# Pooled attention with a feed-forward block: the first batch's steps reordered, its value product turned round

## The chip, the cores and the metric

The kernel runs on one core of one Trainium2 chip. The metric is the device time of one execution in microseconds (us), lower is better; times of several executions are given as their median. TensorE is called PE (its weight loads PEld), VectorE DVE, ScalarE ACT, GpSimd POOL; SP is the engine whose queue issues nearly all DMAs.

## The reference

Four batches of eight heads, 1152 rows of 64 elements. The queries are averaged in pairs, the attention of 576 queries on 1152 keys is formed, and the result goes through a layer norm and a two-layer block with a hidden width of 2048.

```python
q_pool = q.reshape(B, H, S // 2, 2, D).mean(axis=3)
scores = 1.0 / np.sqrt(D) * np.matmul(q_pool, k.transpose(0, 1, 3, 2))
scores = scores - np.max(scores, axis=-1, keepdims=True)
attn = np.exp(scores)
attn = attn / (np.sum(attn, axis=-1, keepdims=True) + 1e-09)
x = np.matmul(attn, v)              # heads side by side: (4, 576, 512)
mu = np.mean(x, axis=-1, keepdims=True)
var = np.mean((x - mu) ** 2, axis=-1, keepdims=True)
xn = (x - mu) / np.sqrt(var + 1e-06) * g_ln
out = x + np.maximum(xn @ w_ch1, 0.0) @ w_ch2
```

## The kernel before

**Steps.** Heads are taken in 16 pairs, each pair in 9 steps of 128 pooled queries, which makes 144 steps. Step i of the main loop (function `step`) issues, in an order written out by hand, a piece of several steps at once: the row maximum of step i (`emit_max`, DVE, line 337), the scores of step i+1 (`emit_s`, PE, line 324: nine matmuls into the three PSUM banks of slot (i+1) mod 2, which are banks 0 to 2 or 3 to 5), the exponential of step i (`emit_exp`, ACT, line 343), the product with V of an earlier step (`emit_pv`, PE) and its evacuation (`evac_pv`: `one` takes the reciprocal of the row sums on DVE, lines 446 to 449, `two` scales the result on ACT, line 453), and one preparation of the next pair's K or Q (`prep_k`, `prep_q`: PE transposes, then a high half by ACT, line 264, and a low half by DVE, line 265). What an engine is given it runs in that order.

**Two ways to turn P.** The product with V needs the exponentials transposed. Steps 36 to 143 do that with a DMA. Steps 0 to 35, the first batch (`on_pe`), do it on PE: `emit_t` (line 376) transposes nine 128x128 float32 blocks back into the banks that held the scores, and `emit_t_copy` (line 382, ACT, in the next step) copies them to SBUF in two parts. `emit_pv` (line 400) then multiplies in float32, with the transposed exponentials as the weight (128x128) and V with a column of ones (65 columns) as what streams through. Each such matmul shows in the trace as two weight loads and two matmuls, so that a step has 18 of each, or 36 in the step that spans two heads. The result goes to columns 128 to 258 of the last bank of slot (i+1) mod 2, the bank into which the scores of step i+1 have just been written.

**Beside it.** The float32 weights of the feed-forward block come in 32 pieces during the first 32 steps: `w_load(m)` (a 512 KB DMA on SP, line 633) in step m, `w_bias` (ACT, line 638) at the end of step m+1, `w_conv` (three DVE operations, queued in `fill` and issued at line 106) from step m+3, `w_sums` (PE, line 665) in even steps, `w_reduce` after every eighth piece. Then `w_splits` has POOL turn them into two float16 parts (lines 238 and 721). `bound` (line 179) and `all_max` (lines 194 to 203) find the scales of a pair's Q, K and V; their PSUM place is the same bank as the result's, in columns 258 to 386. The feed-forward units start some steps after step 36, one to a step (two from step 149 on), and the last 90 us of the span hold little else.

Of the kernel before, what the change touches and what calls it, by code (L numbers as in the profile page):

```python
# [24 lines left out]
def tile_pooled_attention_moe(  # L25
# [93 lines left out]
    def load_q(p, engs, us=(0, 1)):  # L119

        if 0 in us:
            r = raw_p.tile([128, 2, C, 2, D], FP32, tag="qr", name="qr")
        else:
            r = raws[p, "q"]
        for u in us:
            b, hp = divmod(p + u, HP)
            for h in range(2):
                engs[(2 * u + h) % len(engs)].dma_start(  # L128
                    out=r[64 * u:64 * u + 64, h],
                    in_=q[b, 2 * hp + h].rearrange("(p c r) d -> p c r d", c=C, r=2),  # L130
                )
            raws[p + u, "q"] = r
# [51 lines left out]
    def all_max(src, n, then):  # L184

        mx = sm_p.tile([3, 1], FP32, tag="mx3", name="mx3")
        dg = sm_p.tile([3, 3], FP32, tag="dg", name="dg")

        def place():
            return psum[:, 3 * (pv_slot[0] % 2) + 2, 258:386]  # L190

        def one():
            ps = place()
            nc.tensor.transpose(ps[0:n], src, ident)

            def evac():
                nc.vector.tensor_reduce(mx[0:n], ps[0:n], axis=AX.X, op=ALU.max)
                nc.vector.tensor_scalar(dg[0:n, 0:n], ident[0:n, 0:n], mx[0:n], None, op0=ALU.mult)
            return evac

        def two():
            ps = place()
            nc.tensor.matmul(out=ps[:, 0:n], lhsT=ones3[0:n], rhs=dg[0:n, 0:n], start=True, stop=True)
            return lambda: then(ps[:, 0:n])

        return one, two


    reds = deque()

    def scales_reduce(p, a=0, b=3, then=None):
        def end(ps):
# [45 lines left out]
        scaled(vr[:, h], vr[:, h], s)  # L258
        nc.gpsimd.tensor_tensor(vt[:, :, 66:66 + D], vr[:, h], vt[:, :, 0:D], op=ALU.subtract)

    def split_from(ps, s, hi, lo):

        return (
            lambda: nc.scalar.activation(out=hi, in_=ps, func=ACTF.Copy, scale=s),
            lambda: nc.vector.scalar_tensor_tensor(lo, ps, s, hi, op0=ALU.mult, op1=ALU.subtract),  # L265
        )

    def prep_k(p, u):

        kr, kt, s = raws[p, "k"], kt_of(p), pair[p]["s"]  # L270
        ps = bank()
        if u < 2:
            for m in range(4):
                x = kr[:, u, 2 * m:2 * m + 2].rearrange("p c d -> p (c d)")
                nc.tensor.transpose(ps[:, 128 * m:128 * m + 128], x, ident)
            return split_from(ps, s[:, 0:1], kt[:, 0, u, 0:512], kt[:, 1, u, 0:512])
        for h in range(2):
            nc.tensor.transpose(ps[0:64, 128 * h:128 * h + 128], kr[:, h, C - 1], ident)
        x = ps[0:64, 0:256].rearrange("p (h n) -> p h n", h=2)
        return split_from(x, s[0:64, 0:1], kt[0:64, 0, :, 512:640], kt[0:64, 1, :, 512:640])  # L280

    def prep_q(p, u):

        o = 64 * (p % 2)
        qr = raws[p, "q"][o:o + 64].rearrange("p h c r d -> p (h c) (r d)")
        qt, s = qt_of(p), pair[p]["s"]
        ps = bank()
        for m in range(6):
            nc.tensor.transpose(  # L289
                ps[:, 64 * m:64 * m + 64], qr[:, 6 * u + m], ident[o:o + 64, o:o + 64]  # L290
            )
        c = slice(384 * u, 384 * u + 384)
        return split_from(ps[:, 0:384], s[:, 1:2], qt[:, 0, c], qt[:, 1, c])

    PREPS = ((prep_k, 0), (prep_k, 2), (prep_q, 0), (prep_q, 1), (prep_k, 1), (prep_q, 2))

# [14 lines left out]
    def emit_s(i):  # L311
# [3 lines left out]
        if j == 4:  # L315
            parts = [(h, h * C * 64 + 512, 64, 64 * h) for h in range(2)]
        else:
            h = 0 if j < 4 else 1
            parts = [(h, h * C * 64 + 128 * (j if h == 0 else j - 5), 128, 0)]
        for a, (ka, qa) in enumerate(((0, 0), (1, 0), (0, 1))):  # L320

            for r, c0, n, k0 in ((64, 0, 512, 0), (0, 512, 512, 0), (0, 1024, 128, 512)):
# [61 lines left out]
    def emit_pv(i, ps=None):  # L384
# [10 lines left out]
            parts = [(0 if j < 4 else 1, 0, 128, ps[:, 0:65])]  # L395
        if on_pe(i):
            pt = pt.rearrange("p a n -> p (a n)").bitcast(FP32)
            for h, q0, w, dst in parts:
                for u, c in enumerate(ORDER):
                    nc.tensor.matmul(  # L400
                        out=dst, lhsT=pt[:, 128 * u + q0:128 * u + q0 + w], rhs=vt[:, h, c],
                        start=(u == 0), stop=(u == C - 1),
                    )
            return ps
        for h, q0, w, dst in parts:
            for u, c in enumerate(ORDER):
                x = vt[:, h, c]
                hi, lo = pt[:, u, q0:q0 + w], pt[:, C + u, q0:q0 + w]
                for lhsT, rhs in ((hi, x[:, 0:65]), (hi, x[:, 66:130]), (lo, x[:, 0:65])):
# [5 lines left out]
                        skip_group_check=True,  # L415
                    )
        return ps

    pv_slot = [0]
    xb, xh = {}, {}  # L420
# [221 lines left out]
    def w_conv(m):  # L642
# [12 lines left out]
            nc.vector.scalar_tensor_tensor, xi, hi, SIGN, lo,  # L655
            op0=ALU.bitwise_and, op1=ALU.bitwise_or,
        )
        later(lambda: sums.append(lambda: w_sums(part, 2 * c + z, lo)))

    def w_sums(part, u, mag):  # L660

# [8 lines left out]
    def w_reduce(part):  # L670
        while fill:
            drip()
        while sums:
            sums.popleft()()
        m = wmax[:, part:part + 1]
        if part % 2 == 0:

# [54 lines left out]
    def pre(i, fn, *a):  # L732
        early.setdefault(i, []).append((fn, a))

    for p in range(1, NP):
        i0 = (p - 1) * C
        at(max(i0 - 1, 0), load, p, "k", nc.sync)
        at(i0, load, p, "v", nc.sync)
        at(i0 + 1, bound, p, "k")
        if p % 2 == 0:  # L740
            at(i0 - 1, load_q, p, (nc.sync,))
            pre(i0 + 1, pool_q, p, nc.gpsimd)
            at(i0 + 1, dup_q, p, nc.gpsimd)
            at(i0 + 2, bound, p, "q")
        elif p == 1:
            upper = (64, 64)
            pre(0, lambda: nc.gpsimd.memset(state(1)["acc"][0:64, 1:2], 0.0))
            pre(i0 + 1, pool_q, 1, nc.gpsimd, (upper,))
            at(i0 + 1, dup_q, 1, nc.gpsimd, (upper,))
            at(i0 + 2, bound, 1, "q", *upper)  # L750
# [5 lines left out]
        for n in range(2):  # L756
            at(i0 + (5, 7)[n], take_v, p, n)
        for n, (fn, u) in enumerate(PREPS):
            pre(i0 + (4, 5, 6, 6, 7, 8)[n], lambda fn=fn, p=p, u=u: preps.append((fn, p, u)))

    for m in range(32):
        i0 = m
        pre(i0, w_load, m)
        at(i0 + 1, w_bias, m)
        pre(i0 + 3, w_conv, m)
        if m % 8 == 7:
            at(i0 + 3, w_reduce, m // 8)

    this = [0]

# [83 lines left out]
        ready.setdefault(max(n + (2 if on_pe(n) else 4), 3), []).append(n)  # L854
    pieces = deque()

    def some_units(i):
        if preps:
            fn, p, u = preps.popleft()
            evacs.extend(fn(p, u))  # L860
        for _ in range(1 if i < NSTEP + 5 else 2):
            if units and w_done[units[0][0]] >= units[0][1]:
                evacs.extend(units.popleft()[2]())

    def a_piece(i):
        pieces.extend(ready.pop(i, ()))
        for u in range(2 if len(pieces) > 2 else 1):
            if pieces:
                n = pieces.popleft()
                ps = emit_pv(n, bank() if u else None)  # L870
                evacs.extend(evac_pv(n, ps))
                evacs.append(lambda n=n: evacuated(n))

    def step(i):
# [6 lines left out]
        if on_pe(i - 1):  # L881
            emit_t_copy(i - 1)
            steps.pop(i - 1)
        if i + 1 < NSTEP:
            emit_s(i + 1)
            pv_slot[0] = i + 1
        else:
            free_banks[:] = [6, 7, 0, 1, 3, 4]
            pv_slot[0] += 1
        while sums and i % 2 == 0:  # L890
            sums.popleft()()
        flush()
        if live:
            emit_exp(i)
            if not on_pe(i):
                emit_hi(i)
        if 0 <= i - 1 < NSTEP and not on_pe(i - 1):
            emit_lo(i - 1)
# [2 lines left out]
        norm(i)  # L901
        while soon or len(fill) > 3:
            drip()
        if reds:
            evacs.append(reds.popleft()())
        a_piece(i)
        some_units(i)
        if live and on_pe(i):
            emit_t(i)
        for fn, a in todo.pop(i, ()):  # L910
            fn(*a)

    with tc.manual_schedule():
# [14 lines left out]
        make_identity(nc, ident)  # L928
        nc.gpsimd.tensor_copy(ident16, ident)

        for _ in range(70):
            nc.tensor.matmul(out=psum[:, 2, 0:128], lhsT=ident16, rhs=ident16, start=True, stop=True)
        st = state(0)
        nc.vector.memset(st["acc"], 0.0)
# [64 lines left out]
```

## Time and profile before

| | us |
|---|---|
| median of 3 runs | 969.31 (957.99, 969.43, 969.31) |
| span of the profiled execution, first to last instruction | 963.9 |
| PE busy in the span | 880.9 (91%) |
| DVE busy | 627.4 (65%) |
| ACT busy | 549.9 (57%) |
| POOL busy | 346.4 (36%) |
| granted TensorE clock, mean | 0.938 of full speed |

The span is that of one execution under the profiler; the device times of the runs also hold what lies before its first and after its last instruction. No device time is given for the profiled execution itself. Times in the trace count from the span's start. A granted clock of 1.00 is 2.4 GHz and 0.50 is 1.2 GHz.

### The profile page before, as it was taken

What the parts mean: (1) busy time and instruction counts of PE and PEld (TensorE: products, weight loads), DVE (VectorE), ACT (ScalarE), POOL (GpSimd) and SP (SyncE); (2) the same over time, 40 slices, a digit from 0 to 9 for tenths busy, and PEclk for the clock granted to TensorE, in tenths of its full rate; (3) what the DMA queues carried; (4) which work ended last, traced back from release to release, by engine and by line L of the source; (5) the groups of instructions that cost most, each with busy time, mean ns of one, the idle gap of its engine ahead of it and who ended that gap; (6) DMA issues with size and microseconds to landing.
All of it is one profiled execution on the core that took longest, in us unless ns stands there. A gap on an engine that the chain in (4) does not pass through costs nothing.

```text
span 963.9 us, 21832 instructions
## 1 busy us (share of the span) xinstructions
PE 880.9 (91%) x9286; PEld 628.5 (65%) x9286; DVE 627.4 (65%) x1160; ACT 549.9 (57%) x779; POOL 346.4 (36%) x315
## 2 busy tenths in 40 slices
PE   5897988999869899989698999999989999999998
PEld 4676766777747476666474757566765766767665
DVE  4576696767787577757875777678777777542221
ACT  3765465655476677667667677676676766411000
POOL 3002165243579352435543424344534241310000
PEclk7897797968889999999999999999999999999999
DMA  5325152150155988698959596969596886600000
GB/s 156 145 70 183 66 177 69 48 183 1 50 99 106 191 125 171 129 197 133 179 102 209 102 198 129 187 131 174 101 208 118 168 143 116 122 23 12 12 12 22
DMA packets 271665, 114.92 MB, mean 119 GB/s; under 512 B 254928, under 2 KB 254928, under 8 KB 271568
## 3 DMA queue, kind: packets, MB, share of 16 engines
q1 hardware_dynamic: 271216, 112.65, 56.2%
q8 instruction: 72, 1.18, 0.5%
q10 hardware_dynamic: 352, 0.88, 0.3%
q14 instruction: 25, 0.20, 0.1%
HBM read 45.09 MB, written 4.72 MB: 52 GB/s over the span
## 4 chain that ended last, share of the span: by engine, by line
PE 57%; DVE 20%; ACT 9%; DMA 7%; issue 3%; SPq 3%; POOL 0%; ACTq 0%; DVEq 0%; POOLq 0%
PE psum L534 14%; PE psum L565 14%; PE psum L324 8%; PE psum L400 7%; PE psum L411 7%; DVE mx L337 5%; DMA pt<-hl 4%; DVE hl L366 4%; ACT pt L382 3%; PE psum L376 3%; DMA stage<-in_moe_w_ch_dram 2%; DVE ht L548 2%; PE psum L289 2%; SPq L128 2%; DVE kt L265 1%
## 5 line engine op out<-in xcount | busy, mean ns | idle before, releaser
L337 DVE TENSOR_REDUCE mx<-psum 128x1 f32<-128x1152 f32 x144 | 194.4, 1350 | 76.6 <-PE psum L400 39.6
L343 ACT ACTIVATE pe<-psum,nb,sc 128x1152 f32<-128x1152 f32 x144 | 188.9, 1312 | 29.5 <-DVE nb L338 28.2
L565 PE MATMUL psum<-wsl,ht 128*128 128x512 f16 x864 | 199.0, 383 | 0.2 <-DVE ht L548 0.2
L324 PE MATMUL psum<-kt,qt 64*128 64x512 f16 (+3 forms) x1440 | 166.3, 342 | 28.2 <-ACT pt L382 17.0
L534 PEld LDWEIGHTS <-wsl 128*128 128x128 f16 x1920 | 172.8, 99 | 25.1 <-issue 3.0
L534 PE MATMUL psum<-xn,wsl 128*128 128x256 f16 x1536 | 181.2, 277 | 2.1 <-DVE xn L504 1.1
L324 PEld LDWEIGHTS <-qt 64*128 64x128 f16 (+1 forms) x1440 | 70.6, 99 | 114.4 <-issue 76.0
L565 PEld LDWEIGHTS <-ht 128*128 128x128 f16 x864 | 82.5, 99 | 92.2 <-issue 4.3
L357 ACT ACTIVATE hl<-pe 128x1152 f16<-128x1152 f32 x108 | 125.7, 1164 | 19.5 <-DMA pt<-hl 16.2
L453 ACT ACTIVATE xb<-psum,r 128x64 f32<-128x64 f32 x128 | 40.1, 313 | 150.6 <-DVE r L449 142.1
L411 PEld LDWEIGHTS <-pt 128*128 128x128 f16 (+1 forms) x3240 | 108.9, 101 | 22.6 <-issue 22.1
L411 PE MATMUL psum<-vt,pt 128*128 128x65 f16 (+1 forms) x3240 | 120.5, 195 | 0.0
L366 DVE SCALAR_TENSOR_TENSOR hl<-pe,hl 128x1152 f16<-128x1152 f32 x72 | 104.9, 1457 | 0.0
L238 POOL TENSOR_SCALAR pe<-pe 128x1152 f32<-128x1152 f32 x36 | 42.0, 1166 | 153.9 <-ACT hl L357 143.6
L548 DVE SCALAR_TENSOR_TENSOR ht<-psum,ht 128x512 f16<-128x512 f32 x72 | 49.6, 690 | 72.6 <-ACT ht L547 71.8
L547 ACT ACTIVATE ht<-psum 128x512 f16<-128x512 f32 x72 | 42.8, 594 | 93.7 <-PE psum L534 93.3
L400 PE MATMUL psum<-vt,pt 128*128 128x65 f32 (+1 forms) x720 | 96.1, 298 | 0.0
L400 PEld LDWEIGHTS psum<-vt,pt 128*128 128x128 f32 (+1 forms) x720 | 91.9, 213 | 3.6 <-issue 3.4
L364 POOL TENSOR_TENSOR hl<-pe,hl 128x1152 f16<-128x1152 f32 x36 | 85.4, 2373 | 3.0
L382 ACT COPY pt<-psum 128x512 f32<-128x512 f32 x72 | 44.7, 639 | 55.9 <-PE psum L376 55.1
L161 POOL TENSOR_TENSOR qr<-qr 128x1152 f32<-128x1152 f32 (+1 forms) x8 | 22.3, 2786 | 130.2 <-DMA qr<-in_q_dram 94.6
L376 PE MATMUL psum<-ident,pe 128*128 128x128 f32 x324 | 51.7, 315 | 5.1 <-ACT pe L343 4.9
(104 smaller groups left out, 898.6 us busy)
## 6 DMA issues: line engine op xcount, KB each, us to landing
stage<-in_moe_w_ch_dram SPq DMA_DIRECT2D x32, 512.0 KB, 6.7
kr<-in_k_dram SPq DMA_DIRECT2D x16, 576.0 KB, 4.4
qr<-in_q_dram SPq DMA_DIRECT2D x31, 288.0 KB, 5.6
vr<-in_v_dram SPq DMA_DIRECT2D x15, 576.0 KB, 5.0
out_dram<-xb SPq DMA_DIRECT2D x32, 128.0 KB, 2.5
pt<-hl SPq DMA_TRANSPOSE x108, 4.8
vr<-in_v_dram ACTq DMA_DIRECT2D x1, 576.0 KB, 6.1
out_dram<-xh SPq DMA_DIRECT2D x4, 128.0 KB, 3.5
```

Source lines behind the costliest of these rows:

```text
L324: nc.tensor.matmul(out=sp[o:o + w, c0:c0 + n], lhsT=qt[r:r + 64, qa, q0:q0 + w], rhs=kt[r:r + 64, ka, h, k0:k0 + n], start=(a == 0), stop= ...
L337: nc.vector.tensor_reduce(mx, st["s"], axis=AX.X, op=ALU.max)
L343: nc.scalar.activation(out=st["pe"], in_=st["s"], func=ACTF.Exp, scale=pair[i // C]["sc"][:, 0:1], bias=st["nb"],)
L357: nc.scalar.activation(out=hl[:, 0], in_=st["pe"], func=ACTF.Copy, scale=2.0 ** 15)
L364: nc.gpsimd.tensor_tensor(hl[:, 1], st["pe"], hl[:, 0], op=ALU.subtract)
L366: nc.vector.scalar_tensor_tensor(hl[:, 1], st["pe"], 2.0 ** 15, hl[:, 0], op0=ALU.mult, op1=ALU.subtract)
L376: nc.tensor.transpose(st["s"][:, n], st["pe"][:, n], ident)
L382: nc.scalar.copy(st["pt"][:, a:b], st["s"][:, a:b])
L400: nc.tensor.matmul(out=dst, lhsT=pt[:, 128 * u + q0:128 * u + q0 + w], rhs=vt[:, h, c], start=(u == 0), stop=(u == C - 1),)
L411: nc.tensor.matmul(out=dst[:, 0:n], lhsT=lhsT, rhs=rhs, start=(u == 0 and lhsT is hi and n == 65), stop=(u == C - 1 and lhsT is lo), skip_ ...
L534: nc.tensor.matmul(out=ps[:, o:o + n], lhsT=wsl[:, 8 * w + cc, wa, f * 128:f * 128 + 128], rhs=xn[:, xa * KD + cc, 0:n], start=(m == 0), s ...
L565: nc.tensor.matmul(out=ps, lhsT=hv[0][:, ha, f, t * 128:t * 128 + 128], rhs=wsl[:, 8 * w + 4 + f // 2, wa, (f % 2) * DM:(f % 2) * DM + DM] ...
```

## The change

In the first batch's steps the order becomes: product with V of an earlier step, a preparation, the exponential, the scores of step i+1, and then `emit_t`. Columns 0 to 65 of V are now the weight of the product and the transposed exponentials stream through; its result, 65 rows by 128 queries, goes to one of the two spare banks (6 and 7), ACT copies it to SBUF (`nc.scalar.copy(ot, ...)`), and `emit_turn` transposes it on PE into the last bank of slot i mod 2. The reciprocal of that result is taken in the next step behind the maximum (`found`), and the scaling behind the next step's exponential (`scaled_out`). The sums of the weights go to PE in the step in which their bank is that of the scores of step i+1; the bounds go to the bank of slot i. The raw queries get two buffers and are loaded a step earlier; the weights' bias comes two steps later, their conversion one, their reduction one or two. A POOL copy that reads the first pair's scales is put ahead of POOL's first memset in the loop. 110 small matmuls run ahead of the first data, not 70. Assertions and the set `have` add no instruction.

```diff
         if 0 in us:
-            r = raw_p.tile([128, 2, C, 2, D], FP32, tag="qr", name="qr")
+            r = raw_p.tile([128, 2, C, 2, D], FP32, tag="qr", name="qr", bufs=2)
         else:
             r = raws[p, "q"]
...
         def place():
-            return psum[:, 3 * (pv_slot[0] % 2) + 2, 258:386]
+            u = this[0] if on_pe(this[0]) else pv_slot[0]
+            return psum[:, 3 * (u % 2) + 2, 258:386]
 
         def one():
...
-    reds = deque()
+    reds, found = deque(), deque()
 
     def scales_reduce(p, a=0, b=3, then=None):
...
         if on_pe(i):
             pt = pt.rearrange("p a n -> p (a n)").bitcast(FP32)
-            for h, q0, w, dst in parts:
+            for h, q0, w, _ in parts:
                 for u, c in enumerate(ORDER):
                     nc.tensor.matmul(
-                        out=dst, lhsT=pt[:, 128 * u + q0:128 * u + q0 + w], rhs=vt[:, h, c],
+                        out=ps[0:65, q0:q0 + w], lhsT=vt[:, h, c],
+                        rhs=pt[:, 128 * u + q0:128 * u + q0 + w],
                         start=(u == 0), stop=(u == C - 1),
                     )
...
                     )
         return ps
+
+    turned, scaled_out = deque(), deque()
+
+    def emit_turn(n, ot, i):
+
+        j = n % C
+        ps = psum[:, 3 * (i % 2) + 2, 128:258]
+        parts = [(h, 64 * h, 64) for h in range(2)] if j == 4 else [(0, 0, 128)]
+        for h, q0, w in parts:
+            nc.tensor.transpose(ps[0:w, 65 * h:65 * h + 65], ot[:, q0:q0 + w], ident[0:65, 0:65])
+        one, two = evac_pv(n, ps)
+        found.append(one)
+        scaled_out.extend((two, lambda: evacuated(n)))
 
     pv_slot = [0]
...
             op0=ALU.bitwise_and, op1=ALU.bitwise_or,
         )
-        later(lambda: sums.append(lambda: w_sums(part, 2 * c + z, lo)))
+        later(lambda: sums.append((part, lambda: w_sums(part, 2 * c + z, lo))))
 
     def w_sums(part, u, mag):
...
             drip()
         while sums:
-            sums.popleft()()
+            sums.popleft()[1]()
         m = wmax[:, part:part + 1]
         if part % 2 == 0:
...
         early.setdefault(i, []).append((fn, a))
 
+    def behind_scales():
+        nc.gpsimd.tensor_copy(state(1)["acc"][0:64, 1:2], state(0)["sc"][0:64, 0:1])
+        nc.gpsimd.memset(state(1)["acc"][0:64, 1:2], 0.0)
+
     for p in range(1, NP):
         i0 = (p - 1) * C
...
         at(i0 + 1, bound, p, "k")
         if p % 2 == 0:
-            at(i0 - 1, load_q, p, (nc.sync,))
+            at(i0 - 2, load_q, p, (nc.sync,))
             pre(i0 + 1, pool_q, p, nc.gpsimd)
             at(i0 + 1, dup_q, p, nc.gpsimd)
...
         elif p == 1:
             upper = (64, 64)
-            pre(0, lambda: nc.gpsimd.memset(state(1)["acc"][0:64, 1:2], 0.0))
+            pre(0, behind_scales)
             pre(i0 + 1, pool_q, 1, nc.gpsimd, (upper,))
             at(i0 + 1, dup_q, 1, nc.gpsimd, (upper,))
...
             at(i0 + (5, 7)[n], take_v, p, n)
         for n, (fn, u) in enumerate(PREPS):
-            pre(i0 + (4, 5, 6, 6, 7, 8)[n], lambda fn=fn, p=p, u=u: preps.append((fn, p, u)))
+            late = 1 if on_pe(i0) else 0
+            pre(i0 + (4, 5, 6, 6, 7, 8)[n] + late, lambda fn=fn, p=p, u=u: preps.append((fn, p, u)))
 
     for m in range(32):
         i0 = m
         pre(i0, w_load, m)
-        at(i0 + 1, w_bias, m)
-        pre(i0 + 3, w_conv, m)
+        at(i0 + 3, w_bias, m)
+        pre(i0 + 4, w_conv, m)
         if m % 8 == 7:
-            at(i0 + 3, w_reduce, m // 8)
+            at(i0 + (5 if m < 16 else 4), w_reduce, m // 8)
 
     this = [0]
...
     pieces = deque()
 
-    def some_units(i):
+    def a_prep():
         if preps:
             fn, p, u = preps.popleft()
             evacs.extend(fn(p, u))
+
+    def some_units(i):
         for _ in range(1 if i < NSTEP + 5 else 2):
             if units and w_done[units[0][0]] >= units[0][1]:
...
     def a_piece(i):
         pieces.extend(ready.pop(i, ()))
-        for u in range(2 if len(pieces) > 2 else 1):
+        for u in range(2 if len(pieces) > 2 and not on_pe(i) else 1):
             if pieces:
                 n = pieces.popleft()
-                ps = emit_pv(n, bank() if u else None)
+                pt = pts[n]
+                ps = emit_pv(n, bank() if u or on_pe(n) else None)
+                if on_pe(n):
+                    ot = pt.rearrange("p a n -> p (a n)").bitcast(FP32)[0:65, 0:128]
+                    evacs.append(lambda ot=ot, ps=ps: nc.scalar.copy(ot, ps[0:65, 0:128]))
+                    turned.append((n, ot))
+                    continue
                 evacs.extend(evac_pv(n, ps))
                 evacs.append(lambda n=n: evacuated(n))
...
             emit_t_copy(i - 1)
             steps.pop(i - 1)
+        while found:
+            found.popleft()()
+        if on_pe(i):
+            a_piece(i)
+            a_prep()
+            emit_exp(i)
+        while scaled_out:
+            scaled_out.popleft()()
         if i + 1 < NSTEP:
             emit_s(i + 1)
...
             free_banks[:] = [6, 7, 0, 1, 3, 4]
             pv_slot[0] += 1
-        while sums and i % 2 == 0:
-            sums.popleft()()
-        flush()
-        if live:
-            emit_exp(i)
-            if not on_pe(i):
+        while sums and i % 2 == sums[0][0] // 2:
+            sums.popleft()[1]()
+        if on_pe(i):
+            while fill:
+                drip()
+            flush()
+        else:
+            flush()
+            if live:
+                emit_exp(i)
                 emit_hi(i)
         if 0 <= i - 1 < NSTEP and not on_pe(i - 1):
...
         while soon or len(fill) > 3:
             drip()
-        if reds:
+        if on_pe(i):
+            emit_t(i)
+            if reds:
+                found.append(reds.popleft()())
+        elif reds:
             evacs.append(reds.popleft()())
-        a_piece(i)
-        some_units(i)
-        if live and on_pe(i):
-            emit_t(i)
+        while turned:
+            n, ot = turned.popleft()
+            emit_turn(n, ot, i)
+        if not on_pe(i):
+            a_piece(i)
+            a_prep()
+            some_units(i)
         for fn, a in todo.pop(i, ()):
             fn(*a)
...
         nc.gpsimd.tensor_copy(ident16, ident)
 
-        for _ in range(70):
+        for _ in range(110):
             nc.tensor.matmul(out=psum[:, 2, 0:128], lhsT=ident16, rhs=ident16, start=True, stop=True)
         st = state(0)
```

## Rows read from the trace of the kernel before

**Rows 1.** The page's second part: granted clock in 40 slices of 24.1 us, in tenths.

```profile
PEclk7897797968889999999999999999999999999999
```

**Rows 2.** Windows: stretch, its length, busy us (instructions) of each engine, granted clock, DMA share, GB/s.

```profile
23.00:256.00 233.00, 205.70 (x1589) 164.38 (x1590) 161.48 (x310) 135.02 (x214) 75.88 (x55) 0.84 0.30 99
256.00:964.00 708.00, 661.00 (x7581) 453.21 (x7579) 455.64 (x831) 408.56 (x554) 263.21 (x245) 0.98 0.66 125
...
44.26:71.85 27.59, 25.55 (x241) 20.54 (x239) 21.87 (x47) 18.91 (x31) 0.00 (x0) 1.00 0.20 61
79.06:106.91 27.85, 23.35 (x114) 18.42 (x114) 14.58 (x27) 11.34 (x18) 5.17 (x5) 0.58 0.31 115
114.30:134.55 20.25, 18.08 (x172) 14.22 (x171) 19.77 (x29) 12.69 (x21) 17.43 (x12) 1.00 0.32 104
195.38:221.28 25.90, 24.29 (x136) 19.71 (x135) 14.83 (x31) 14.17 (x23) 10.20 (x7) 0.58 0.54 171
```

**Rows 3.** Timeline of DVE, row maxima of steps 1, 34, 35 and 36: start, us, instruction.

```profile
23.04 1.35 DVE L337 TENSOR_REDUCE mx<-psum 128x1 f32<-128x1152 f32 x1
...
243.10 1.34 DVE L337 TENSOR_REDUCE mx<-psum 128x1 f32<-128x1152 f32 x1
251.71 1.35 DVE L337 TENSOR_REDUCE mx<-psum 128x1 f32<-128x1152 f32 x1
255.74 1.36 DVE L337 TENSOR_REDUCE mx<-psum 128x1 f32<-128x1152 f32 x1 [0.52 <-PE psum L400]
```

**Rows 4.** Waits, 22 to 236 us: who for whom, us in total, times, longest.

```profile
DVE mx L337 <- PE psum L400: 38.3, 17, 4.9
...
PE psum L324 <- ACT pt L382: 15.8, 36, 4.2
```

**Rows 5.** Timeline of PE in a step at the full clock.

```profile
227.59 1.15 PE L376 MATMUL psum<-ident,pe 128*128 128x128 f32 x9
...
229.51 0.97 PE L324 MATMUL psum<-kt,qt 64*128 64x512 f16 x8 [0.28 <-ACT pt L382]
...
230.54 2.09 PEld L400 LDWEIGHTS psum<-vt,pt 128*128 128x128 f32 x18
230.57 2.20 PE L400 MATMUL psum<-vt,pt 128*128 128x65 f32 x18
```

**Rows 6.** Timeline around the two long stretches at the half clock.

```profile
81.69 0.66 ACT L638 ACTIVATE wsl<-stage 128x512 f32<-128x512 f32 x1 [4.46 <-DMA stage<-in_moe_w_ch_dram]
...
82.87 0.37 PE L324 MATMUL psum<-kt,qt 64*128 64x512 f16 x1 [4.15 <-ACT pt L382]
...
199.56 4.10 PE L400 MATMUL psum<-vt,pt 128*128 128x65 f32 x18
```

**Rows 7.** Timeline of PE (two rows); groups by shape, 23 to 256 us (five).

```profile
114.10 0.38 PE L278 MATMUL psum<-ident,kr 128*64 128x128 f32 x2
...
244.95 4.16 PE L400 MATMUL psum<-vt,pt 128*64 128x65 f32 x36
...
L343 ACT ACTIVATE pe<-psum,nb,sc 128x1152 f32<-128x1152 f32 x36 | 47.2, 1312 | 2.3 <-DVE nb L338 2.3
...
L382 ACT COPY pt<-psum 128x512 f32<-128x512 f32 x35 | 20.5, 585 | 50.6 <-PE psum L376 50.6
L453 ACT ACTIVATE xb<-psum,r 128x64 f32<-128x64 f32 x28 | 8.9, 316 | 31.4 <-DVE r L449 31.4
...
L264 ACT ACTIVATE kt<-psum,s 128x512 f16<-128x512 f32 x7 | 4.8, 683 | 0.0
...
L265 DVE SCALAR_TENSOR_TENSOR kt<-psum,s,kt 128x512 f16<-128x512 f32 x7 | 5.2, 745 | 0.0
```

**Rows 8.** Timeline of the start.

```profile
1.71 5.54 PE L932 MATMUL psum<-ident 128*128 128x128 f16 x70 [1.71 <-POOL ident L929]
...
12.31 2.61 POOL L161 TENSOR_TENSOR qr<-qr 64x1152 f32<-64x1152 f32 x1 [2.40 <-DMA qr<-in_q_dram]
...
12.47 2.48 DVE L231 TENSOR_SCALAR s<-s 128x3 f32<-128x3 f32 x1
```

More of the change, by code (lines that the diff above doesn't have):

```diff
@@ L259, in take_v, with split_from, low @@
         nc.gpsimd.tensor_tensor(vt[:, :, 66:66 + D], vr[:, h], vt[:, :, 0:D], op=ALU.subtract)
[L261 to L266, printed above, removed]
+    def split_from(what, ps, s, hi, lo):
+        def low():
+            nc.vector.scalar_tensor_tensor(lo, ps, s, hi, op0=ALU.mult, op1=ALU.subtract)
+            have.add(what)
+        return (lambda: nc.scalar.activation(out=hi, in_=ps, func=ACTF.Copy, scale=s), low)
+    have = set()
     def prep_k(p, u):
@@ L275, in prep_k @@
                 nc.tensor.transpose(ps[:, 128 * m:128 * m + 128], x, ident)
-            return split_from(ps, s[:, 0:1], kt[:, 0, u, 0:512], kt[:, 1, u, 0:512])
+            return split_from((p, "k", u), ps, s[:, 0:1], kt[:, 0, u, 0:512], kt[:, 1, u, 0:512])
         for h in range(2):
@@ L279, in prep_k @@
         x = ps[0:64, 0:256].rearrange("p (h n) -> p h n", h=2)
-        return split_from(x, s[0:64, 0:1], kt[0:64, 0, :, 512:640], kt[0:64, 1, :, 512:640])
+        return split_from((p, "k", 2), x, s[0:64, 0:1], kt[0:64, 0, :, 512:640], kt[0:64, 1, :, 512:640])
     def prep_q(p, u):
@@ L292, in prep_q @@
         c = slice(384 * u, 384 * u + 384)
-        return split_from(ps[:, 0:384], s[:, 1:2], qt[:, 0, c], qt[:, 1, c])
+        return split_from((p, "q", u), ps[:, 0:384], s[:, 1:2], qt[:, 0, c], qt[:, 1, c])
     PREPS = ((prep_k, 0), (prep_k, 2), (prep_q, 0), (prep_q, 1), (prep_k, 1), (prep_q, 2))
@@ L319, in emit_s @@
             parts = [(h, h * C * 64 + 128 * (j if h == 0 else j - 5), 128, 0)]
+        for h, q0, w, o in parts:
+            need = {(p, "k", h), (p, "k", 2), (p, "q", q0 // 384), (p, "q", (q0 + w - 1) // 384)}
+            assert need <= have, (i, need - have)
         for a, (ka, qa) in enumerate(((0, 0), (1, 0), (0, 1))):
```

## The prediction

> **What bounds it now.** I first read the clock over the whole span. It is below 1.00 in nearly every slice of the first quarter and at full speed behind it [rows 1]. The windows put numbers on that: the stretch of the first batch, 23 to 256 us, had PE busy for 205.7 of 233 us at a clock of 0.84, the other 708 us 661.0 at 0.98 [rows 2]. The change is all in the start and the first batch, so I look at that stretch next. From the maximum of step 1 to that of step 36 it is 35 steps in 232.7 us (23.04 to 255.74), 6.65 us each [rows 3].
>
> These steps are not alike. Three kinds come out of the windows, whose ends are starts of row maxima [rows 2, 3]:
> - *cold*, at or near the 1.2 GHz level: 79.06 to 106.91 (3 steps, clock 0.58), 195.38 to 221.28 (3 steps, 0.58) and 243.10 to 251.71 (1 step). Seven steps in 62.4 us, 8.91 us each. PE is then 84 to 94% busy, because its work takes twice as long: one product with V is 4.10 us there [rows 6] and 2.20 us at full clock [rows 5].
> - *plain*, at 2.4 GHz with POOL idle: 44.26 to 71.85, 5 steps, 5.52 us each, PE 93% and DVE 79% busy.
> - *split*, with POOL turning weights: 114.30 to 134.55, 3 steps, 6.75 us each, DVE 19.77 of 20.25 us busy. Here DVE is the bound, not PE.
>
> Then the waits. The row maximum waited 38.3 us for the product with V, which writes the bank that the maximum reads; the scores waited 15.8 us, some 0.4 us a step, for ACT's copy of the transposed block [rows 4]. The longest single stop is one behind the other: ACT's bias sat 4.46 us until a weight DMA landed, the copy queued behind it came late, and PE stood for 4.15 us at 82.87 us [rows 6]. The first long cold stretch begins right there.
>
> **The change, part by part.** *The product.* Before, 18 weight loads of 128 columns take 2.09 us and 18 matmuls of 65 columns 2.20 us, side by side [rows 5]: 0.116 us a pass, set by the load. After, a pass loads 65 columns and streams 128. No row shows float32 128 columns streamed in a true product. From below: the shape of the two-head step, 64 columns of weight and 65 streamed, took 4.16 us for 36 at the half clock, 0.058 us each at full [rows 7], so neither side of the new pass costs less than that half. From above, 65 streamed columns cost at most that 0.058, so 128 cost at most 0.114 and the load of 65 hides beside it; the nearest transpose (64 columns loaded, 128 streamed) is two in 0.38 us, of which some 0.11 is the second [rows 7]. Without any overlap it would be 0.058 + 0.114 = 0.172. I take 0.114, as the rows of 5 overlap: 18 x 0.114 = 2.05 us, the same as now. The product itself gains nothing.
>
> The Trainium skill (TensorE: Matmul & The Clock Gate, Part 3, "What overlaps and what doesn't") says that weight loads run beside matmuls in flight only if they use other rows of the array. Both use all 128 rows here. By that rule the old product would have taken 18 x (0.116 + 0.058) = 3.1 us, and the measured 2.20 us speaks against it [rows 5]; by it the new one would be 3.1 us too.
>
> *Added.* One transpose a step on PE (128 columns loaded, 65 streamed): between 0.06 and 0.3 us, taken 0.15. One copy of 65x128 on ACT: between the scaling of 64 columns, 0.316, and the copy of 512, 0.585 [rows 7]; I take 0.35. ACT has the room: 135 of 233 us busy [rows 2].
>
> *Order on PE.* Between `emit_t` and the next scores now come the turn, the product and a preparation, about 2.7 us, so the copies (1.3 us) end under them and the 0.4 us wait goes. PE needs per step: 1.15 (transposes) + 0.15 + 2.05 + up to 0.6 (preparation) + 1.2 (scores) = 5.15 us. What is late next: the product's bank 6 or 7 is no longer one that the maximum reads, so the maximum starts with the end of the scores, but DVE must first finish the low half of the preparation. That makes a ring: exponential 1.31, scaling 0.32, the new copy 0.35, high half 0.68, low half 0.75, maximum 1.36 and back to the exponential, 4.77 us, plus five handoffs at an estimated 0.1: 5.3 us [rows 3, 7]. So a plain step becomes 5.3, not 5.52. The new wait in it is that of the scores of step i+2 on the scaled output (same bank); behind it on PE queue the sums and `emit_t`. It costs nothing as long as exponential and scaling end before PE's 5.15 us are round, and most of a microsecond if DVE is late.
>
> *Split steps.* DVE's bound is untouched: 6.7 us. Three of the four weight quarters fall in this stretch; at 12 POOL pieces of nearly 5 us each that is some ten steps.
>
> *Weights and queries.* The bias two steps later gives each DMA some 10 us more, which covers the 4.46 us stop; the query load has a buffer of its own, so SP no longer holds weight and V loads behind it, and coming a step earlier it is ahead of one weight load (a few us of DMA with two steps of slack). The later conversion and reduction move the last split about one step; the first unit that needs it is 16 units behind, so nothing waits. The sums in the other bank remove a wait of PE for DVE in the second half of the weights; I count nothing for it beyond the plain step.
>
> *Start.* At 12.47 us a DVE operation on three columns took 2.48 us beside POOL's add of 2.61 us [rows 8]. The added POOL copy holds that add back until the scales are there: about 2.3 us of the opening chain. POOL's add, its copy and the bound behind it then come some 2.5 us later and are wanted steps later. Forty more small matmuls at 5.54/70 us are 3.2 us; they run before the first data reaches PE at about 10.4 us and cost nothing, or up to 1 us without that cover.
>
> *The clock.* It is the largest term and the least sure. If the stop behind the bias goes, so should the first long cold stretch; the second began with smaller gaps, in which PE waited for DVE's bound and ACT's copy, that the new order also hides. I take that 2 of the 7 cold steps stay.
>
> **The sum.** 2 x 8.91 + 23 x 5.3 + 10 x 6.7 = 206.7 us against 232.7: 26.0 saved, and 2.3 at the start. Behind step 36 the order is as before: 708 us stay. The span goes from 963.9 to 935.6. The median stands 5.4 us above the span, which suits what lies around a span, so I take 969.3 - 28.3 = 941 us.
>
> **Rivals.**
> - *Better:* no cold step stays and the ring closes under PE: 25 x 5.1 + 10 x 6.0 = 187.5, 45 saved, 922 us. For it: the rows of plain steps with PE at 93%. Against: DVE full in split steps.
> - *The clock stays as it is:* 7 x 8.91 + 19 x 5.3 + 9 x 6.7 = 223.4, 9.3 + 2.3 saved, 958 us, no difference that can be told. For it: once cold, PE stayed cold for three steps although it was 94% busy in the second stretch [rows 2].
> - *The scores' new wait takes the place of the old ones:* a plain step of 6.0 and a split step of 7.2 make 25 x 6.0 + 10 x 7.2 = 222, 956 us. For it: DVE is late in split steps, and the wait sits behind ACT's exponential.
> - *Slower:* a pass costs load plus stream, 0.172 us, twice that when cold. PE's step is 5.15 + 18 x 0.058 = 6.2 us, a cold one 8.91 + 2.1 = 11.0, a split one 6.9. With the clock as it is: 7 x 11.0 + 19 x 6.2 + 9 x 6.9 = 256.9, 24.2 lost, 2.3 won: 991 us. It decides from about 0.02 us a pass over my 0.114: the 11.6 us saved with the clock as it is, and 2.9 us of slack in plain steps (19 x 0.15), over 18 x (28 + 2 x 7) passes at full clock. Against it: the overlap in rows 5. The rule of the Trainium skill (TensorE: Matmul & The Clock Gate) told above is this rival's.
>
> **Chances.** Forecast 0.45, better 0.22, clock 0.13, new wait 0.12, slower 0.08. About 2%, or 19 us, is what a measurement of this kernel can tell from none: its three runs spread over 11. The range reaches from below the better case to above the two that end near 957: 914 to 964. Faster by over 2% (under 950) is the better case and most of the forecast, 0.67; within 2% 0.25; slower 0.08.
>
> **What the new trace would show.** Right: in the stretch up to step 36 a clock over 0.95 with few slices at half, plain steps near 5.3 us, 18 float32 matmuls of the product in about 2.05 us with short weight loads under them, no wait of the maximum for the product, no stop of ACT's bias for a DMA, the scale's DVE operation near 0.2 us. Wrong: 18 matmuls in 3 us; scores that wait for ACT's scaling by half a microsecond or more a step; cold stretches as long as before; or a change behind step 36, where I expect none.

## The result and the profile after

The changed kernel takes 909.41 us, the median of four runs (905.75 to 911.05), against 963.65 for the kernel before, now with four runs (956.1 to 969.43). The ratio is 0.9437 (95% interval 0.9371 to 0.9503): 5.6% faster. I had forecast 941 and a range that ended at 914. The sign was right, the size half of what came. The ratios here and in the table of experiments are formed from fast runs alone.

The profiled execution took 911.05 us with a span of 909.3, so 1.75 us lie around a span. My 5.4 was too much; with 1.75 the same sum would have given 937, which changes nothing.

The span fell by 54.6 us. The row maxima of steps 1 and 36 cut it in three, as they did ahead of the prediction [rows 3]. Timeline of DVE after:

```profile
22.50 1.35 DVE L344 TENSOR_REDUCE mx<-psum 128x1 f32<-128x1152 f32 x1
...
215.47 1.35 DVE L344 TENSOR_REDUCE mx<-psum 128x1 f32<-128x1152 f32 x1
```

| stretch | before | after | won | forecast |
|---|---|---|---|---|
| start, up to the maximum of step 1 | 23.0 | 22.5 | 0.5 | 2.3 |
| steps 1 to 36 | 232.7 | 193.0 | 39.7 | 26.0 |
| behind step 36 | 708.2 | 693.9 | 14.3 | 0 |

The clock of the page and the windows of the middle stretch, of one plain step and of three split steps, to be read beside [rows 1, 2]:

```profile
PEclk8899999998898999999799999999999999999999
```

```profile
22.50:215.47 192.97, 166.46 (x1627) 135.62 (x1626) 167.00 (x309) 140.05 (x246) 72.44 (x53) 0.97 0.36 115
53.66:58.26 4.60, 4.56 (x51) 3.66 (x50) 4.04 (x10) 4.18 (x8) 0.00 (x0) 1.00 1.02 221
94.17:116.06 21.89, 18.20 (x182) 15.11 (x180) 20.91 (x30) 13.65 (x24) 17.33 (x12) 0.92 0.34 113
```

The clock of the first batch went from 0.84 to 0.97, and the long cold stretches are gone; what is left near the lower level is the first two steps (0.55 from 22.50 to 30.38 us). Of the 35 intervals between row maxima, 21 are under 5.7 us and 4.56 us in the mean; 14 are over 6.2 and 6.94 in the mean. The short intervals are plain steps; in the one of the second window PE, DVE and ACT are all nearly full (4.56, 4.04 and 4.18 of 4.60 us). The long ones are mostly split steps (POOL works for more than half of the interval in 11 of the 14), as in the third window (three steps, 7.30 us each): DVE is busy for 20.91 of 21.89 us, nearly full as it was before [rows 2].

One plain step in the timeline of all engines, from one row maximum to the next, with the transposes ahead of it:

```profile
43.52 1.20 PE L383 MATMUL psum<-ident,pe 128*128 128x128 f32 x9
...
44.35 1.35 DVE L344 TENSOR_REDUCE mx<-psum 128x1 f32<-128x1152 f32 x1
...
44.56 0.22 PE L435 MATMUL psum<-ident,pt 65*128 65x65 f32 x1
44.56 1.95 PEld L407 LDWEIGHTS psum<-pt,vt 128*65 128x65 f32 x18
44.62 2.13 PE L407 MATMUL psum<-pt,vt 128*65 128x128 f32 x18
...
46.04 1.31 ACT L350 ACTIVATE pe<-psum,nb,sc 128x1152 f32<-128x1152 f32 x1 [0.53 <-DVE r L467]
...
46.58 0.38 PE L282 MATMUL psum<-ident,kr 128*64 128x128 f32 x2
...
47.25 0.30 ACT L474 ACTIVATE xb<-psum,r 128x64 f32<-128x64 f32 x1
...
47.45 0.25 ACT L902 COPY pt<-psum 65x128 f32<-65x128 f32 x1
47.59 0.47 ACT L268 ACTIVATE kt<-psum,s 64x256 f16<-64x256 f32 x1
47.60 0.76 PE L331 MATMUL psum<-kt,qt 64*128 64x128 f16 x7 [0.32 <-ACT xb L474]
...
48.10 0.48 DVE L265 SCALAR_TENSOR_TENSOR kt<-psum,s,kt 64x256 f16<-64x256 f32 x1
...
48.58 1.18 PE L383 MATMUL psum<-ident,pe 128*128 128x128 f32 x9
48.76 1.36 DVE L344 TENSOR_REDUCE mx<-psum 128x1 f32<-128x1152 f32 x1 [0.18 <-PE psum L686]
```

The turned product takes 2.13 us for 18 passes, and the next work on PE starts 1.96 us after it, 0.109 us a pass: the same as before, as forecast [rows 5]. The new wait is there too: seven of the scores' matmuls stand 0.32 us for the scaling on ACT (line 474). Over the stretch these are, in the view of waits:

```profile
PE psum L331 <- ACT xb L474: 19.5, 15, 2.1
...
PE psum L331 <- ACT xh L474: 6.1, 3, 2.5
```

At the start the DVE operation that stood beside POOL's add is short, 0.17 us instead of 2.48 [rows 8]:

```profile
12.43 0.17 DVE L232 TENSOR_SCALAR s<-s 128x3 f32<-128x3 f32 x1
```

### The profile page after: what moved, and what is told of

It is laid out like the page before. It is cut to its first block, busy times and chain, and to the rows that moved or that the text cites. A ratio compares the mean times of both kernels' runs of the same rounds, so it can differ in the third digit from the quotient of the medians.

```text
span 909.3 us, 22075 instructions
## 1 busy us (share of the span) xinstructions
PE 842.0 (93%) x9366; PEld 600.8 (66%) x9366; DVE 631.2 (69%) x1160; ACT 556.0 (61%) x815; POOL 345.3 (38%) x316
## 4 chain that ended last, share of the span: by engine, by line
PE 50%; DVE 30%; ACT 10%; DMA 5%; issue 3%; POOL 1%; SPq 0%; ACTq 0%; POOLq 0%; DVEq 0%
PE psum L555 16%; PE psum L586 14%; DVE mx L344 8%; PE psum L331 7%; PE psum L419 6%; DVE hl L373 5%; DVE stage L106 3%; ACT pe L350 2%; DVE wsl L106 2%; PE psum L383 2%; PE psum L407 2%; DMA pt<-hl 2%; DVE kt L265 2%; DVE ht L569 2%; ACT kt L268 2%
## 5 line engine op out<-in xcount | busy, mean ns | idle before, releaser
L555 PEld LDWEIGHTS <-wsl 128*128 128x128 f16 x1920 | 171.8, 99 | 23.8 <-issue 2.3
L331 PE MATMUL psum<-kt,qt 64*128 64x512 f16 (+3 forms) x1440 | 156.0, 333 | 33.8 <-ACT xb L474 24.5
L331 PEld LDWEIGHTS <-qt 64*128 64x128 f16 (+1 forms) x1440 | 65.0, 98 | 110.9 <-issue 76.1
L419 PEld LDWEIGHTS <-pt 128*128 128x128 f16 (+1 forms) x3240 | 107.7, 101 | 22.5 <-issue 22.1
L373 DVE SCALAR_TENSOR_TENSOR hl<-pe,hl 128x1152 f16<-128x1152 f32 x72 | 107.1, 1488 | 0.0
L407 PE MATMUL psum<-pt,vt 128*65 128x128 f32 (+1 forms) x720 | 79.6, 267 | 0.0
L407 PEld LDWEIGHTS psum<-pt,vt 128*65 128x65 f32 x720 | 74.0, 142 | 0.0
L265 DVE SCALAR_TENSOR_TENSOR qt<-psum,s,qt 128x384 f16<-128x384 f32 x48 | 29.6, 616 | 40.5 <-ACT qt L268 40.4
L265 DVE SCALAR_TENSOR_TENSOR kt<-psum,s,kt 128x512 f16<-128x512 f32 (+1 forms) x48 | 31.5, 657 | 37.5 <-ACT kt L268 37.4
```

The costliest lines, as they stand in the source:

```text
L331: nc.tensor.matmul(out=sp[o:o + w, c0:c0 + n], lhsT=qt[r:r + 64, qa, q0:q0 + w], rhs=kt[r:r + 64, ka, h, k0:k0 + n], start=(a == 0), stop= ...
L373: nc.vector.scalar_tensor_tensor(hl[:, 1], st["pe"], 2.0 ** 15, hl[:, 0], op0=ALU.mult, op1=ALU.subtract)
L407: nc.tensor.matmul(out=ps[0:65, q0:q0 + w], lhsT=vt[:, h, c], rhs=pt[:, 128 * u + q0:128 * u + q0 + w], start=(u == 0), stop=(u == C - 1),)
L419: nc.tensor.matmul(out=dst[:, 0:n], lhsT=lhsT, rhs=rhs, start=(u == 0 and lhsT is hi and n == 65), stop=(u == C - 1 and lhsT is lo), skip_ ...
L555: nc.tensor.matmul(out=ps[:, o:o + n], lhsT=wsl[:, 8 * w + cc, wa, f * 128:f * 128 + 128], rhs=xn[:, xa * KD + cc, 0:n], start=(m == 0), s ...
```

## The experiments

Each run stands against runs of the kernel before on the same chip. "Steps" is the time between the maxima of steps 1 and 36 with its clock, "rest" what follows to the end of the span, both of one profiled execution each.

| kernel | median us | ratio to before (95%) | steps | clock | rest |
|---|---|---|---|---|---|
| before | 963.65 | 1 | 232.7 | 0.84 | 708.2 |
| changed | 909.41 | 0.944 (0.937 to 0.950) | 193.0 | 0.97 | 693.9 |
| changed, again | 909.9 | 0.948 (0.943 to 0.953) | 192.3 | 0.95 | 691.1 |
| single_q | 937.31 | 0.976 (0.968 to 0.983) | 205.4 | 0.92 | 705.0 |
| two_q_late | 928.08 | 0.965 (0.957 to 0.972) | 201.7 | 0.93 | 705.8 |
| before_two_q | 940.02 | 0.978 (0.970 to 0.986) | 224.1 | 0.86 | 686.8 |
| weights_early | 911.11 | 0.949 (0.942 to 0.955) | 194.8 | 0.94 | 691.1 |
| sums_old | 920.65 | 0.960 (0.953 to 0.967) | 205.6 | 0.92 | 687.4 |
| unflipped | 919.91 | 0.957 (0.951 to 0.963) | 208.0 | 0.89 | 687.6 |
| copied | 901.62 | 0.936 (0.930 to 0.942) | 185.0 | 0.93 | 687.9 |
| copied, again | 900.28 | 0.939 (0.934 to 0.944) | 189.3 | 0.89 | 685.7 |
| flip_only | 1070.13 | 1.112 (1.105 to 1.119) | 333.1 | 0.77 | 711.6 |
| scaled_first | 912.76 | 0.948 (0.941 to 0.955) | 194.2 | 0.95 | 694.0 |
| bank_only | 942.26 | 0.980 (0.972 to 0.988) | 233.9 | 0.82 | 686.2 |
| order_alone | 940.49 | 0.982 (0.976 to 0.989) | 206.5 | 0.86 | 705.1 |
| order_queries | 920.14 | 0.962 (0.953 to 0.970) | 200.5 | 0.87 | 690.0 |

**The query loads.** `load_q` is called for every second pair of all 16, so the buffer and the earlier load also act behind step 36, where I had counted "the order is as before". First the changed kernel without them:

```diff
-            r = raw_p.tile([128, 2, C, 2, D], FP32, tag="qr", name="qr", bufs=2)
+            r = raw_p.tile([128, 2, C, 2, D], FP32, tag="qr", name="qr")
-            at(i0 - 2, load_q, p, (nc.sync,))
+            at(i0 - 1, load_q, p, (nc.sync,))
```

> The changed kernel with one query buffer, loaded in the step of before. Theory 1 (SP's queue stood behind the query loads in every second pair, and the second buffer freed it): the 14 us behind step 36 are lost again, 923 us, with SP waiting some 19 us for the query transposes; steps 1 to 36 nearly as in the changed kernel. Rival (the 14 us are chance between two executions): 909 us, 694 us behind step 36.

It lost 28 us, twice what I expected: the rest is back at 705.0, and the steps lost 12.4 as well. Waits of the whole span and the timeline of its worst stop:

```profile
POOL qr L161 <- DMA qr<-in_q_dram: 115.0, 7, 51.3
...
ACT qt L179 <- POOL qr L161: 11.1, 2, 6.3
```

```profile
74.77 2.61 POOL L161 TENSOR_TENSOR qr<-qr 128x1152 f32<-128x1152 f32 x1 [51.27 <-DMA qr<-in_q_dram]
...
77.40 1.16 ACT L179 ACTIVATE qt<-qr 128x1152 f16<-128x1152 f32 x1 [6.28 <-POOL qr L161]
...
79.12 1.16 ACT L389 COPY pt<-psum 128x512 f32<-128x512 f32 x2
79.74 1.23 PE L331 MATMUL psum<-kt,qt 64*64 64x512 f16 x4 [4.80 <-ACT pt L389]
```

Read it from the bottom: PE stood 4.80 us for ACT's copy, the copy was queued behind ACT's bound of the queries, the bound waited 6.28 us for POOL's add, and that for the query DMA. In the kernel before the same PE stop of 4.15 us stood behind ACT's bias [rows 6]. I take both for the same late traffic on one queue, seen through whichever instruction happens to be first in ACT's line: in the kernel before, SP issued four query loads at 72.40 us and the next weight DMA at 74.91, just ahead of that stop.

Is it the buffer or the earlier start? With two buffers, loaded as late as before (only the second half of the diff above):

> The changed kernel with two query buffers but the load in the step of before. Theory 1 (it is the buffer, for SP no longer stands behind a load that waits): 909 to 913. Rival (the earlier start of the load matters, for POOL and ACT wait for the queries): 920 or more, with an ACT stop near 74 us.

928: some 9 of the 28 us come back with the buffer and the other 19 only with the earlier start. SP no longer waits for the buffer (17.0 us in `single_q`), but the rest is 705.8 as with one buffer. So SP's queue behind the loads was the smaller part; the queries have to be there when POOL's add comes. Waits behind step 36 in `two_q_late`, where nothing has changed for POOL, nor for PE's wait for ACT's bounds:

```profile
POOL qr L161 <- DMA qr<-in_q_dram: 39.5, 5, 9.7
...
PE psum L195 <- ACT kt L179: 14.6, 6, 3.8
```

The changed kernel has 7.8 and 5.4 us there. The earlier start with one buffer was not run. The other way round, the kernel before with nothing but the two edits:

```diff
-            r = raw_p.tile([128, 2, C, 2, D], FP32, tag="qr", name="qr")
+            r = raw_p.tile([128, 2, C, 2, D], FP32, tag="qr", name="qr", bufs=2)
-            at(i0 - 1, load_q, p, (nc.sync,))
+            at(i0 - 2, load_q, p, (nc.sync,))
```

> The kernel before with two query buffers and the load a step earlier, nothing else. Theory 1: 14 us less behind step 36, and perhaps the second long cold stretch, whose queue stood behind a query load too: 945 to 952 us. Rival (chance): 964 us.

940.02, 21 us less than the kernel before beside it (961.15), and more than the 945 to 952 I expected: the cheapest edit of all. Across the table the rest is 685 to 694 us in the eleven rows with an early load and a second buffer, and 705 to 712 in the five that lack one or both; that was no chance.

**The weights' later bias.** I had put the first cold stretch down to the stop for a weight DMA.

```diff
-        at(i0 + 3, w_bias, m)
-        pre(i0 + 4, w_conv, m)
+        at(i0 + 1, w_bias, m)
+        pre(i0 + 3, w_conv, m)
-            at(i0 + (5 if m < 16 else 4), w_reduce, m // 8)
+            at(i0 + 3, w_reduce, m // 8)
```

> The changed kernel with the weights' bias, conversion and reduction in the steps of before. Theory 1 (the stops for weight DMAs set off the cold stretches): one or two stops of 2 to 5 us return and with them cold stretches, 920 to 930 us. Rival (the new order alone hides them): 909 within 5 us.

911.11: no difference that this measurement shows. Once the query loads are out of the way the weights come in time with two steps less: here, as in `before_two_q`, no wait of the bias for a weight DMA is left.

**The order.** The order of the change in the kernel before, all else as before; the product is unturned and ACT copies its result from the spare bank to SBUF, so that reciprocal and scaling can come in the next step (the edit of `copied` below):

> The kernel before with the order of the change in the first batch alone: unturned product in the spare bank, copied to SBUF by ACT, reciprocal and scaling in the next step; sums, bounds, weights, start and query loads as before. Theory (the order is worth some 20 us by itself, the gains add): 935 to 945. Rival (without the query loads the stops for DMAs and the cold stretches eat it): 950 to 962.

> The same with two query buffers loaded a step earlier. Theory (additive): 20 to 28 us below the run above, 910 to 920. Rival (the order needs the banks of sums and bounds too): 925 to 935.

940.49 and 920.14: by the ratios that is 17 and 37 us under the kernel before. The query loads alone were 21, so the two add. In `order_alone` the rest stays at 705.1, and the stop for the DMA is still there (PE 6.01 us at 82.13). What the order itself removes could have been the maximum's wait for the product, 38.3 us [rows 4], or PE's wait for the copies. To tell, the kernel `before_two_q` with the product in a spare bank and no other order:

```diff
-                ps = emit_pv(n, bank() if u else None)
+                ps = emit_pv(n, bank() if u or on_pe(n) else None)
```

> The kernel before with two query buffers (940) and the first batch's product in the spare bank, in the order of before and unturned. If the maximum's wait for the product is what the new order removes, most of the remaining gain is here: 915 to 925. If it is the copies' end that TensorE stands for, the step stays near 6 us: 933 to 943.

942.26, nothing won over 940.02, though the maximum's wait for the product (22.8 us in `before_two_q`) is gone from the list. It was a wait of an engine that was not late; the order is what pays. Only one of its parts is told apart by a run, in the first two runs on the product below.

**The turned product.** Three runs. In the first the product is as before, in the spare bank, and reciprocal and scaling follow in the same step:

```diff
-                        out=ps[0:65, q0:q0 + w], lhsT=vt[:, h, c],
-                        rhs=pt[:, 128 * u + q0:128 * u + q0 + w],
+                        out=dst, lhsT=pt[:, 128 * u + q0:128 * u + q0 + w], rhs=vt[:, h, c],
...
-                if on_pe(n):
+                if False:
                     ot = pt.rearrange("p a n -> p (a n)").bitcast(FP32)[0:65, 0:128]
```

> The changed kernel with the product as before: the transposed exponentials are the weight, V streams, the result goes to the spare bank and is scaled from there in the same step, without copy and transpose. Theory 1 (the order makes the gain, the turned product none of it): 909 within 6 us, steps 1 to 36 within 193 +- 6 us, clock of the first batch above 0.95. Rival (the turned product is what keeps TensorE at 2.4 GHz): cold stretches come back, the first batch's clock falls under 0.90, 925 to 935 us.

It took 919.91 us, 10 more than the changed kernel and between the theory and the rival, with the clock at 0.89, which looked like the rival. But the run changed two things: the scaling in the same step made ACT wait for the reciprocal:

```profile
ACT xb L473 <- DVE r L469: 46.2, 25, 4.1
...
PEld psum L407 <- ACT xb L473: 11.3, 8, 3.4
```

So a second one, `copied`, keeps the places: ACT copies the 128x65 result to SBUF where the change copies 65x128, and reciprocal and scaling read it there in the next step.

```diff
+                if on_pe(n):
+                    w, m = (64, 130) if n % C == 4 else (128, 65)
+                    ot = pt.rearrange("p a n -> p (a n)").bitcast(FP32)[:, 0:130]
+                    evacs.append(
+                        lambda ot=ot, ps=ps, w=w, m=m: nc.scalar.copy(ot[0:w, 0:m], ps[0:w, 0:m])
+                    )
+                    turned.append((n, ot))
...
-            nc.tensor.transpose(ps[0:w, 65 * h:65 * h + 65], ot[:, q0:q0 + w], ident[0:65, 0:65])
-        one, two = evac_pv(n, ps)
+        one, two = evac_pv(n, ot)
```

> The changed kernel with the product as before (exponentials as weight), its 128x65 result copied from the spare bank to SBUF by ACT where the changed kernel copies 65x128, and reciprocal and scaling in the same places of the next step, from SBUF: the turn is gone, nothing else. Theory 1 (the turned product gains nothing by itself; the first unflipped run lost its 10 us by ACT waiting for the reciprocal in the same step): 909 or less; the scores' wait of 25 us for the scaling is gone too, 895 to 909. Rival (the turned product keeps the clock): cold stretches of 40 us or more in steps 1 to 36, 915 to 922.

> The kernel with the unturned product copied to SBUF once more, beside the changed kernel on the same chip. If the 8 us that it was ahead are the scores' wait for the scaling, it is again 6 to 10 us ahead, about 901; if they were chance, the two are within 3 us.

> The changed kernel, unaltered, as the partner of the run above: 906 to 911 us.

901.62 and, beside the changed kernel on one chip, 900.28 against 909.9: the best kernel here, 8 to 10 us ahead of the change. The turned product costs that much; it wins no time. `copied` is also some 18 us ahead of `unflipped`, from which it differs only by the place of reciprocal and scaling and the copy that this needs. So taking them a step later is likely to be most of what the order is worth, though no run tests that in `order_alone`. In `copied` the scores no longer wait for the scaling. The source view of their line in both, what ended PE's idle time before it, the changed kernel first:

```profile
  ACT xb L474: 19.5, 15
  ACT xh L474: 6.1, 3
```

```profile
  issue: 9.2, 29
  DVE mx L198: 0.5, 1
  ACT pt L389: 0.5, 2
```

The last, the kernel before with the product turned and nothing else:

> The kernel before with only the product turned: V as weight into a spare bank, ACT's copy, the transpose into the last bank of slot i mod 2, in the order of before. Theory 1 (no gain in the product; but the maximum of step i+1 no longer waits for it, as the bank is another): some 5 to 15 us less than before, 945 to 955, cold stretches about as long. Rival (the turned product raises the clock): steps 1 to 36 with under 30 us at the half clock, 930 to 940.

A wide miss: 1070 us. The turn writes columns 128 to 258 of a bank whose first 128 columns the exponential of the same step reads, and in the old order that exponential is still to run. That the shared bank is the reason I read from the code. The waits of steps 1 to 36 (22 to 356 us) show PE standing for that exponential; line 428 is the turn, and the wait of its matmuls is 63.5 us in 30 times:

```profile
PEld psum L428 <- ACT pe L343: 69.1, 31, 3.8
```

With such a gap in most steps the clock fell to 0.77 and the steps took 333 us. In the changed order the turn comes behind `emit_t`, which waits for the exponential anyway. So the turned product needs the order; the order does not need it.

**The sums and bounds.** I had counted nothing for the sums "beyond the plain step", and had not priced the bounds.

```diff
-        while sums and i % 2 == sums[0][0] // 2:
+        while sums and i % 2 == 0:
...
-            u = this[0] if on_pe(this[0]) else pv_slot[0]
+            u = pv_slot[0]
```

> The changed kernel with the weights' sums in even steps only and the bounds in the bank of the next slot, as before. Theory: the sums of the second half of the weights then stand behind the maximum that reads their bank, some 2 us in a handful of steps, 914 to 922. Rival (hidden in the other waits): 909 within 3 us.

920.65, 11 us more, all in the steps (205.6 against 192 to 193). One new wait of the maximum is that for the bounds in its bank, which the changed kernel does not have:

```profile
DVE mx L344 <- PE psum L204: 11.3, 7, 1.8
```

**The scaling ahead of the exponential**, to end the scores' wait without undoing the turn:

```diff
-            emit_exp(i)
         while scaled_out:
             scaled_out.popleft()()
+        if on_pe(i):
+            emit_exp(i)
```

> The changed kernel with the scaling of the last result ahead of the exponential on ACT. If the scores' wait for the scaling sets the step, 8 to 20 us less, 890 to 902. If the ring of exponential, preparation and maximum sets it, the exponential comes some 0.3 us later and the time is 909 to 918.

912.76, nothing won. Of PE's 25.6 us of waits for the scaling 12.8 are left, but ACT, with the exponential queued behind, now stands for the reciprocal (22 to 215 us):

```profile
ACT xb L474 <- DVE r L470: 40.6, 28, 3.7
```

## Why the prediction was off

*Right.* The product costs the same turned or not (0.109 us a pass against my 0.114), so the rival in which load and stream add up is out; weight loads of all 128 rows run beside matmuls here, 1.95 beside 2.13 us. The long cold stretches went. The DVE operation at the start is short. The long steps stayed mostly DVE's: 6.94 us in the mean, forecast 6.7.

*The step that failed most* is "Behind step 36 the order is as before: 708 us stay". I read the load's two edits as part of the first batch, though the loop over pairs that calls `load_q` runs to the last pair. And inside the batch I priced them as a queue relieved, at no number of their own. Alone they are worth 21 us, undone 28. The clue was in the trace before, in the waits behind 256 us, which I had not read:

```profile
POOL qr L161 <- DMA qr<-in_q_dram: 38.3, 4, 10.1
...
PE psum L194 <- ACT kt L179: 15.1, 5, 3.6
```

The same two behind step 36 (215.47 us) after the change:

```profile
POOL qr L161 <- DMA qr<-in_q_dram: 7.8, 3, 2.7
...
PE psum L195 <- ACT kt L179: 5.4, 6, 2.0
```

POOL's add no longer stands for the queries, and PE stands some 10 us less for ACT's bounds, out of the 14.3 us that the stretch became shorter. The runs show that the earlier load does this; how the one wait leads to the other is not shown.

*Mis-sized terms.* "So a plain step becomes 5.3" came out at 4.56. The ring was summed with the largest preparation, 0.68 and 0.75 us [rows 7], and then used for every plain step. Groups of the high halves by shape, 22.50 to 215.47 us:

```profile
L268 ACT ACTIVATE qt<-psum,s 128x384 f16<-128x384 f32 x11 | 6.4, 584 | 0.6 <-PE psum L293 0.5
...
L268 ACT ACTIVATE kt<-psum,s 128x512 f16<-128x512 f32 x7 | 4.8, 689 | 0.8 <-PE psum L279 0.6
...
L268 ACT ACTIVATE kt<-psum,s 64x256 f16<-64x256 f32 x4 | 1.9, 474 | 0.0
```

Only seven of the 35 steps have the largest one. Three of them are among the 21 short steps; these, which also hold the bounds, take 5.50 us in the mean, more than my 5.3 (the one from 38.91 to 44.35 us takes 5.44). The other 18, with a smaller preparation or none, take 4.40. So the sum came near the fullest kind of plain step and was wrong for the rest. In the step above, whose two halves take 0.47 and 0.48, overlap does its part too: I summed shown durations and added five handoffs of 0.1 that no row gave, but on one engine the next instruction begins before the shown end of the last. ACT's copy starts 0.20 us after the scaling of 0.30, the high half 0.14 after the copy of 0.25. The same on PE: 1.10 us from `emit_t` (43.52) to the product, the turn in between, and 1.96 from there to the preparation, where I had 1.30 and 2.05. Over 21 steps that is 21 x 0.74 = 15.5 us. "2 of the 7 cold steps stay" was two too many, at most 2 x (8.91 - 4.56) = 8.7 us; against these stand 14 long steps where I had ten. "I count nothing for it beyond the plain step", of the sums, should have been about 11 with the bounds. The scores' wait for the scaling was to cost nothing unless DVE was late; at 25.6 us over 35 steps, 0.73 a step, it reached what I had named as a sign of being wrong, and `copied` prices it, with the turn, at 8 to 10 us.

*The causes of the clock.* I named the stop for the weight DMA. The runs say that no single part did it: the clock of the first batch is 0.86 with the query loads alone or the order alone, 0.87 with both, 0.92 with all but the banks of sums and bounds, 0.95 to 0.97 with all. And it is no goal of its own: `copied` has 0.89 to 0.93 and is faster. The turned product does go with a slightly higher clock: over the whole span 0.967 to 0.974 in the ten executions of the changed kernel, 0.950 to 0.963 in the ten of `copied`. Why is open.

So the gain, 54 us by the first ratio and 50 by the second, is by runs: query loads 21 to 28, the order 17 to 20, the banks of sums and bounds 11, the turn minus 8 to 10, the weights' timing nothing that shows. The start was not run alone: the maximum of step 0 comes 3.1 us earlier (18.43 against 21.53 us), and most is given back by step 1, whose scores now stand behind the last preparation. How much the start's edits bring shows in the runs with the new order: step 1's maximum comes at 26.59 and 27.55 us in the two with the old start, at 21.8 to 23.8 in the ten with the new one. That is some 4 us, and with them the parts add up to 43 to 55.

## What to carry to other kernels

Ask of every edited line which iterations run it, before asking what stage it was meant for; the largest single gain here was a load that runs in all pairs. Price each kind of step by what it holds, not all of them by the fullest, and by start-to-start times on each engine, for the shown durations overlapped by 0.1 to 0.2 us an instruction. When an operation is reversed to fit a new order, test the order with the old operation: here the version that only copies the unturned result is the fastest.

## What I had not expected of the hardware

Once at 1.2 GHz, PE could stay there at high load: the kernel before was 94% busy from 195 to 221 us and had a clock of 0.58 in it [rows 2]. The Trainium skill (TensorE: Matmul & The Clock Gate, Part 1) tells that activity releases the throttle; these rows show a busy engine that was not released for some 20 us, while it ran float32 transposes, float32 products of 65 streamed columns and float16 scores.
